# The gather of the special columns behind one more POOL sum, and the three stages of the special frequency two groups later

## The chip, the cores and the metric

The kernel runs on one core of one Trainium2 chip. The core has five engines with instruction queues of their own: TensorE (PE; its weight loads are shown as PEld), VectorE (DVE), ScalarE (ACT), GpSimd (POOL) and SyncE (SP), the last of which only issues DMAs here. Sixteen DMA engines move the data. The metric is the device time of one execution in microseconds (us); smaller is better.

## The reference

One transformer-like block on x of 2048 x 640 in bfloat16, with a spectral filter in place of attention:

```python
mod = (silu(c) @ w_mod).reshape(1, 6, 1, 640)     # sa, ca, ga, sb, cb, gb
h = layernorm(x) * (1 + ca) + sa
X = rfft2(h) * (w_r + 1j * w_i)                   # 2048 x 321 frequencies
x = x + ga * irfft2(X)
h = layernorm(x) * (1 + cb) + sb
x = x + gb * ((silu(h @ w_gate) * (h @ w_up)) @ w_down)   # hidden size 1728
```

## The kernel before, in words

All arithmetic of the two transforms is done as matrix products with tables of cosines and sines. The kernel is one long function; its order of instructions on every engine is the order in which the Python lines run, written out by hand (no planner moves anything). Five parts follow one another:

1. **Forward transform** (up to about 32 us of the profile): layer norm, products with table M (L404) and table R (L413, L415); the result A lies in tile rA.
2. **Join** (about 32 to 60 us): the loop `for g in range(NG + 1)` over 21 groups of column frequencies, four columns each. For group g+2 the function `mix` makes four products (L583) into PSUM, DVE multiplies them with the filter (`prod`, L607, two instructions a group); one or two groups later `stage_b` adds the products up on PE (L615), ACT copies the sum (L618), `stage_c` transforms back in the first step (L645), and ACT or DVE puts the result into tiles Em and Er, which lie in rE (L654). For the odd groups 3 to 17 (`PRE`) POOL adds the two halves of the product first (`presum`, L624, into rE), which halves the work of `stage_b` for that group. Beside these sums POOL adds filter tables (`wsum`, L424) and scales tables for the next part (L785, L791).
3. **Stage one** (about 60 to 80 us): for 16 row tiles t, products of Em and Er with Htab (L728, L737), a copy by ACT (L732), products with RI (L1273, L1276), and a DVE instruction (L1278) that adds x and gives x1. While it runs, the second layer norm of the first two tiles is made (DVE L864), transposed by a DMA (`ln2_tr`, L878, into rW), and scaled and shifted by POOL and ACT (`ln2_mod`, L886, L892).
4. **Gate and up products** of the first chunk of two tiles: `gu13` (L1090, called at t = 15 and waiting for `ln2_mod`), then `gu_plain` (L1102), then the down product (L980).
5. The other three chunks of 4, 4 and 6 tiles, with products saved by Strassen-like sums (L1132, L1003).

**The special frequency.** Rows with frequency 128 times a whole number need a table of their own (Ks). Their path runs through all groups at once. `sp_gather` (L663, nine small POOL additions) collects one element column out of each of the transposed tiles and adds SA, and puts it into B2sp. Then come three stages, each a PE part (`sp_mm`) and an evacuation by DVE (`sp_ev`): stage 0 is three products out of B2sp (L676) and three DVE multiplications (L697); stage 1 is four products (L681) and two DVE copies (L702); stage 2 is four products (L685, L689), two DVE copies (L705), and two DMA stores from SP, L706 and L707, which write row 127 of Em and of Er. Stage one reads that row with its very first product (L728). The three stages use odd g alone, and so the same columns of PSUM that the products of that group leave free.

**Where these stand before the change.** In the loop, `sp_gather` is called at the head of g = 6; on POOL it stands behind the sum for group 7 and ahead of the sum for group 9 (which the loop issues at g = 7). Stages 0, 1, 2 stand at g = 9, 11, 13 (`SPG`): the PE part ahead of the products of group g+2; the DVE part of stages 1 and 2 ahead of the two multiplications of group g+2, that of stage 0 behind them.

**What feeds and follows them.** The gather reads four tiles that DMA transposes fill (L543), issued one after another by SP; the last one writes into rM (columns 64 to 79). Behind the two stores L706 and L707 the SP queue holds, in this order: five loads of the down weights into rA (L822 twice, L824, L825, L826), two small loads of the last gate and up columns (L829, L830), three loads of gate and up weights into rW (L834: gate columns 0 to 511, gate 512 to 1663, up 0 to 511), then the transpose L878 of the second layer norm, and two more up loads (L834). POOL issues a load of gate weights by itself during stage one (L912).

The lines of the loop on which this rests:

```python
        SPG = (9, 11, 13)
        for g in range(NG + 1):
            if g == 6:
                sp_gather()
            if 1 < g < NG - 2:
                if g in SPG:
                    sp_mm(SPG.index(g), g)
                xps = mix(g + 2)
                if g in SPG and SPG.index(g) in (1, 2):
                    sp_ev(SPG.index(g), g)
                prod(g + 2, xps, 0)
                prod(g + 2, xps, 1)
                ...
                if g in SPG and SPG.index(g) not in (1, 2):
                    sp_ev(SPG.index(g), g)
            if g + 2 in PRE:
                presum(g + 2)
```

Of the kernel before, what the change touches and what calls it, by code (L numbers as in the profile page):

```python
# [166 lines left out]
def adaln_block_kernel(ctx, tc, A_x, A_w_r, A_w_i, B_x, B_w_gate, B_w_up, B_w_down, c, w_mod, out):  # L167
# [165 lines left out]
    if True:  # L333
        def bn(ti, n=1, mid=None):
            for i in range(ti, ti + n):
                for k in range(2):
                    nc.vector.bn_stats(bn6a[:, i % 2, k, :], x_sb[:, i, 320 * k:320 * k + 320])  # L337
                    if i == ti + 1 and k == 0 and mid is not None:
                        if mid in (4,6,8):
                            xhat(mid, nc.vector)  # L340
                            xhat(mid + 1, nc.vector)
                        else:
                            xpair(mid)
            for i in range(ti, ti + n):
                nc.vector.bn_aggr(mv[:, i, :], bn6a[:, i % 2])
# [15 lines left out]
        def xpair(lo):  # L361
            nc.gpsimd.tensor_scalar(nmean[:, lo:lo + 2], mv[:, lo:lo + 2, 0], -1.0, 0.0, ALU.mult, ALU.add)
            xhat(lo, nc.gpsimd)
            xhat(lo + 1, nc.vector)

        def xhat(ti, eng):
            o, xi, r = xhs[ti // 2 % 3][:, ti % 2], x_sb[:, ti, :], rstd[:, ti:ti + 1]
            if eng is nc.vector:
                eng.tensor_scalar(o, xi, mv[:, ti, 0:1], r, ALU.subtract, ALU.mult)  # L369
            else:  # L370
                eng.tensor_scalar(o, xi, nmean[:, ti:ti + 1], r, ALU.add, ALU.mult)
# [164 lines left out]
    if True:  # L536
# [22 lines left out]
        def t2_pe(slot):  # L559
            ls = groups[slot] + (groups[4] if slot == 3 else [])  # L560
            n = len(ls)
            tp = banks(slot % 2, 1, [8, 128], BF16)
            for i, l in enumerate(ls):
                nc.tensor.transpose(tp[:, i, :], A_sb[:, l].rearrange("p t k c r -> p (t k c r)"), identb[:])
            B2 = (rM.cut(38400 + 1024 * slot, [n, 128]) if slot < 2 else rM.cut(10240 + 1024 * (slot - 2), [n, 128]))
            if slot == 0:
                nc.scalar.copy(B2[:, 0:2], tp[:, 0:2, :])
                nc.scalar.copy(B2[:, 2:4], tp[:, 2:4, :])
            else:
                nc.scalar.copy(B2[:], tp[:, :n, :])  # L570
            spec.append((B2, 4, slice(ls[0], ls[0] + 4)))
            if n > 4:
                spec.append((B2[:, 4:6], 2, slice(0, 81, 80)))
            for i, l in enumerate(ls):
                B2of[l] = (B2, i)

        def mix(g):
            ls = groups[g]
            n = len(ls)
            xps = banks(2 + 2 * (g % 2), 2, [4, 256])  # L580
            for i, l in enumerate(ls):
                B2, j = B2of[l][0:2]
                nc.tensor.matmul(xps[:, i, 0:192], lhsT=B2[:, j, :], rhs=KS2, start=True, stop=True)  # L583
                if i == 0:
                    for c5 in {8: (0,), 10: (1,), 12: (2,), 14: (3,), 16: (4,), 18: (5, 6), 20: (7, 8, 9)}.get(g, ()):
                        mod_col(psum[:, 3 + 2 * (g % 2), 448 + c5:449 + c5], wm_r[:, :, 1 + c5 // NC5], c5 % NC5)
            return xps
# [11 lines left out]
        def prod(g, xps, hl, v0=0, v1=3):  # L599
            ls = groups[g]  # L600
            n = len(ls)
            if g not in PPs:
                PPs[g] = rM.cut(1536 * (g % 4), [3, 2, NT, 2, n])
            xv = xps[:, :n, 0:192].rearrange("p i (v h k m) -> p v h k m i", v=3, h=2, k=NT)
            st = ls[1] - ls[0]
            in1 = _rev(Wt, (160 - ls[0] if hl else ls[0]) + WP * v0, [[WP, v1 - v0], [321, NT], [160, 2], [-st if hl else st, n]])
            nc.vector.tensor_tensor(PPs[g][:, v0:v1, hl], xv[:, v0:v1, hl], in1, ALU.mult)  # L607
# [53 lines left out]
        def sp_gather():  # L661
            for B2, n, ls in spec:
                nc.gpsimd.tensor_tensor(B2sp[:, ls], B2[:, 0:n, 127], SA[:, ls], ALU.add)  # L663
# [4 lines left out]
        def sp_mm(i, g):  # L668
            b = 2 + 2 * (g % 2)
            if i == 3:  # L670
                for j in range(10):
                    nc.tensor.matmul(psum[:, 1, 320:401], lhsT=SL[:, j // 2, j % 2, :], rhs=Rp[:, j // 2, 81 * (j % 2):81 * (j % 2) + 81],
                                     start=(j == 0), stop=(j == 9))
            elif i == 0:
                for v in range(3):
                    nc.tensor.matmul(gap(81, v, 64, b), lhsT=B2sp[:, 0:81], rhs=Kstab[:, 64 * v:64 * v + 64], start=True, stop=True)  # L676
            elif i == 1:
                for h in range(2):
                    ls = slice(41 * h, 41 + 40 * h)
                    for ps in (1, 0):  # L680
                        nc.tensor.matmul(gap(128, h, ls.stop - ls.start, b), lhsT=PPsp[:, 64 * ps:64 * ps + 128], rhs=identb[0:81, ls],  # L681
                                         start=(ps == 1), stop=(ps == 0))
            elif i == 2:
                for e in range(2):
                    nc.tensor.matmul(gap(128, 0, 1, b), lhsT=Kstab[:, 320 + 128 * e:448 + 128 * e], rhs=Y2sp[:, 80 * e:80 * e + 1],  # L685
                                     start=(e == 0), stop=(e == 1))
                for h, ls in enumerate((slice(1, 40), slice(40, 80))):
                    o = gap(128, h, 40, b)[:, 1 - h:40]
                    nc.tensor.matmul(o, lhsT=Kstab[:, 192:320], rhs=Y2sp[:, ls], start=True, stop=True)  # L689
# [52 lines left out]
        PPs, Y2s, Qs = {}, {}, {}  # L742
        PRE = (3, 5, 7, 9, 11, 13, 15, 17)
        LAGS = range(3, 18)
        SPG = (9, 11, 13)
        t2_pe(0)
        t2_pe(1)
        wsum(0, 16, 8, nc.gpsimd)
# [13 lines left out]
        for g in range(NG + 1):  # L762
            if g == 9:
                nc.gpsimd.tensor_copy(sgnc[:], Kstab[:, 576:577])
            if g == 6:
                sp_gather()
            if 1 < g < NG - 2:
                if g in SPG:
# [6 lines that stand above are left out]
                if g == 2:  # L775
                    wsum(32, 48, 8, nc.gpsimd)
# [4 lines that stand above are left out]
            if g in (10, 12):  # L781
                wsum(64, 80, 8 * (10, 12).index(g), nc.gpsimd)
            if g in (14, 18):
                h4 = slice(4 * (14, 18).index(g), 4 * (14, 18).index(g) + 4)
                nc.gpsimd.tensor_scalar(sgn_H[:, h4, 1], sgn_H[:, h4, 0], sgnc[:, 0:1], 1.0, ALU.mult, ALU.mult)  # L785
            if g == NG - 3:
                nc.vector.tensor_copy(modcols[:, 2, :], psum[:, 3, 448:453])
                nc.vector.tensor_scalar_add(one_p_cb[:], psum[:, 3, 453:458], 1.0)
            if g in (16, 17):
                i = 1 - (16, 17).index(g)  # L790
                nc.gpsimd.tensor_tensor(RI[:, i], RI[:, i], ga_bc[:], ALU.mult)  # L791
            if 0 < g < 3:
                ga_mod(320 * (2 - g), 8 - g)
            for b in (g - 1, g):
                if 0 <= b < NG and (b in LAGS) == (b < g):
                    if b == 4:
                        tp = sp_w()
                        sp_mm(3, 4)
                    Y2s[b] = stage_b(b, PPs.pop(b))
                    if b == 4:  # L800
                        sp_wc(tp)
                        sp_ev(3, 4)
            if g in (7, 9):
                i = (7, 9).index(g)
                turn(64, i, 6 + i, act)
            if g == 0:
                stage_a(3)
            for u, gs in enumerate(units):
                if gs[-1] + (1 if gs[0] >= NG - 2 else 2) == g:
                    stage_c(u)  # L810
                    evac(u)
            if g == NG - 1:
                for c5 in range(NC5):
                    mod_col(psum[:, 3, 192 + c5:193 + c5], wm_r[:, :, 3], c5)
# [596 lines left out]
```

## Time and profile before

| | |
|---|---|
| median of 3 runs | 247.27 us (246.79 to 247.45) |
| the profiled execution's own time | 247.35 us |
| its span, first to last instruction | 245.6 us |
| granted TensorE clock | 0.998 |
| busy: PE, PEld, DVE, ACT, POOL | 236.9, 186.0, 205.5, 170.2, 78.8 us |
| share of the span on the chain that ended last | PE 79%, DVE 7%, POOL 5%, DMA 4% |

An execution takes 1.75 us more than its span. A row of the timeline gives the start in us, the duration in us, the engine, the line, the operation and what it writes and reads, how many instructions are drawn together, and in brackets how long the engine had been idle and what ended that. SP's rows are the issues of DMAs; the data moves later. In the rows of stretches of time, the numbers behind each engine are its busy us in the stretch, and the last two are the mean busy share of the DMA engines (over 1 where several packets are open on one engine) and what they moved in GB/s.

### The profile page before, as it was taken

Reading aid. Unit: us, or ns where it says so; the run is one execution under the profiler, and the core shown is the slowest. Engines: PE = TensorE matmul, PEld = TensorE weight load, DVE = VectorE, ACT = ScalarE, POOL = GpSimd, SP = SyncE. Lnnn points to the kernel's source line nnn. Section 1 sums busy time; section 2 is a strip of 40 time slices with the busy share of each in tenths; the row PEclk is TensorE's granted clock in tenths of the full one; section 3 lists DMA queues with packets and bytes.
Section 4 is the critical chain, followed back from the end, with each engine's and each line's share of the span. In section 5 each row is a group of like instructions: output and inputs, shape, how many; then the busy total and the mean of one; then the engine's idle time right before and its main releaser. Section 6 shows DMA issues by size and latency. Waiting matters only on the chain.

```text
span 245.6 us, 5940 instructions
## 1 busy us (share of the span) xinstructions
PE 236.9 (96%) x2221; PEld 186.0 (76%) x2221; DVE 205.5 (84%) x485; ACT 170.2 (69%) x338; POOL 78.8 (32%) x122
## 2 busy tenths in 40 slices
PE   8899999899999999999999999999999999999994
PEld 2777889799997887788887778887765665666773
DVE  4898988797699995989989968788998777789864
ACT  3898877899997887588864588765247787773220
POOL 3637997698615414002004400001422000004400
PEclk9999999999999999999999999999999999999999
DMA  7999989989999899600005110202411000000111
GB/s 207 373 342 305 349 183 157 261 240 355 327 317 256 166 245 189 138 1 3 0 3 107 56 56 0 56 1 41 91 31 56 0 0 1 3 1 0 56 53 53
DMA packets 44142, 31.19 MB, mean 127 GB/s; under 512 B 21873, under 2 KB 41810, under 8 KB 44114
## 3 DMA queue, kind: packets, MB, share of 16 engines
q1 hardware_dynamic: 42176, 26.15, 41.2%
q0 software_dynamic: 1376, 4.26, 7.6%
q10 hardware_dynamic: 562, 0.41, 0.5%
q8 instruction: 17, 0.28, 0.5%
q14 instruction: 11, 0.09, 0.1%
HBM read 23.49 MB, written 2.62 MB: 106 GB/s over the span
## 4 chain that ended last, share of the span: by engine, by line
PE 79%; DVE 7%; POOL 5%; DMA 4%; issue 3%; ACT 0%; SPq 0%; DVEq 0%; POOLq 0%
PE psum L1132 36%; PE psum L1003 19%; PE psum L1102 6%; PE psum L980 3%; DMA rW<-rL 3%; DVE bn6a L337 3%; PE psum L615 2%; PE psum L583 2%; PE psum L1090 2%; PE psum L404 1%; DMA rX<-in_A_x_dram 1%; DVE rE L369 1%; PE psum L645 1%; POOL rL L1285 1%; DVE rM L607 1%
## 5 line engine op out<-in xcount | busy, mean ns | idle before, releaser
L1132 PEld LDWEIGHTS <-rW 128*128 128x128 bf16 (+1 forms) x429 | 42.0, 98 | 12.6
L1132 PE MATMUL psum<-rW 128*128 128x256 bf16 (+1 forms) x247 | 42.2, 287 | 0.0
L1029 POOL TENSOR_TENSOR rM<-rM,rL 128x320 f32<-128x320 f32 x6 | 5.4, 906 | 96.6 <-ACT rL L1028 96.6
L1003 PEld LDWEIGHTS <-rE 128*128 128x128 f16 (+1 forms) x196 | 19.0, 97 | 7.8
L1003 PE MATMUL psum<-rE 128*128 128x320 f16 (+1 forms) x147 | 22.9, 299 | 0.0
L607 DVE TENSOR_TENSOR rM<-psum,rW 128x384 bf16<-128x384 f32 (+2 forms) x42 | 20.4, 544 | 2.8 <-PE psum L583 2.8
L1170 ACT COPY rX<-psum 128x384 f32<-128x384 f32 (+2 forms) x27 | 14.0, 520 | 7.5 <-PE psum L1132 7.4
L1132 PEld LDWEIGHTS <-rE 128*128 128x128 f16 x156 | 15.3, 98 | 4.7
L1163 ACT COPY rH<-psum 128x384 f32<-128x384 f32 (+2 forms) x27 | 14.0, 517 | 7.0 <-PE psum L1132 6.3
L1167 DVE TENSOR_TENSOR rH<-psum,rM 128x512 bf16<-128x512 f32 (+1 forms) x24 | 15.0, 624 | 4.1 <-PE psum L1132 2.2
L1186 ACT ACTIVATE rL<-psum 128x384 bf16<-128x384 f32 (+2 forms) x27 | 14.4, 533 | 5.4 <-PE psum L1132 3.4
L1171 DVE TENSOR_TENSOR rX<-psum,rX 128x384 f32<-128x384 f32 (+2 forms) x27 | 16.3, 604 | 1.6 <-ACT rX L1170 1.4
L1157 ACT COPY rM<-psum 128x384 f32<-128x384 f32 (+2 forms) x27 | 13.9, 516 | 3.7 <-PE psum L1132 3.7
L1278 DVE SCALAR_TENSOR_TENSOR rM<-psum,rX 128x640 f32<-128x640 f32 x16 | 13.1, 821 | 3.8 <-PE psum L737 2.5
L1132 PE MATMUL psum<-rW,rE 128*128 128x256 bf16 (+1 forms) x78 | 15.6, 290 | 0.0
L1132 PE MATMUL psum<-rE,rY 128*128 128x256 f16 (+1 forms) x78 | 15.6, 290 | 0.0
L1187 ACT ACTIVATE rL<-rX 128x384 bf16<-128x384 f32 (+2 forms) x27 | 15.1, 558 | 0.0
L337 DVE BATCH_NORM_STATS2 bn6a<-rX 128x6 f32<-128x320 bf16 x30 | 13.1, 480 | 2.2 <-DMA rX<-in_A_x_dram 2.2
L1102 PE MATMUL psum<-rW 128*128 128x256 bf16 x130 | 14.4, 273 | 0.0
L972 DVE TENSOR_TENSOR rA<-psum,rM 128x320 bf16<-128x320 f32 (+1 forms) x27 | 12.1, 472 | 2.4 <-PE psum L980 2.3
L1102 PEld LDWEIGHTS <-rW 128*128 128x128 bf16 x130 | 12.7, 98 | 1.4
L424 POOL TENSOR_TENSOR rW<-rW 128x256 bf16<-128x256 bf16 x20 | 13.4, 700 | 0.7 <-DVE rW L393 0.5
(235 smaller groups left out, 640.0 us busy)
## 6 DMA issues: line engine op xcount, KB each, us to landing
rM<-in_w_mod_dram SPq DMA_DIRECT2D x4, 800.0 KB, 8.3
out_dram<-rA SPq DMA_DIRECT2D x31, 80.0 KB, 1.6
rX<-in_A_x_dram SPq DMA_DIRECT2D x6, 320.0 KB, 5.6
rA<-in_B_w_down_dram SPq DMA_DIRECT2D x2, 960.0 KB, 5.4
rY<-in_B_w_gate_dram POOLq DMA_DIRECT2D x2, 832.0 KB, 7.7
rW<-in_B_w_gate_dram SPq DMA_DIRECT2D x1, 1440.0 KB, 10.5
rW<-in_A_w_i_dram SPq DMA_DIRECT2D x2, 642.0 KB, 10.8
rW<-in_A_w_r_dram SPq DMA_DIRECT2D x2, 642.0 KB, 10.2
```

What stands on the lines that cost most here:

```text
L337: nc.vector.bn_stats(bn6a[:, i % 2, k, :], x_sb[:, i, 320 * k:320 * k + 320])
L607: nc.vector.tensor_tensor(PPs[g][:, v0:v1, hl], xv[:, v0:v1, hl], in1, ALU.mult)
L1003: nc.tensor.matmul(o, lhsT=lhs[rows(k), k], rhs=rhs[rows(k), k], start=start and k == ks[0], stop=stop and k == ks[-1], skip_group_check=True)
L1102: nc.tensor.matmul(gu[u], lhsT=Wgu[:, u, c5, ff * 128:(ff + 1) * 128], rhs=h2T[:, :, c5, :], start=(c5 == 0), stop=(c5 == NC5 - 1))
L1132: nc.tensor.matmul(o[:, f], lhsT=w, rhs=b, start=(start and f == 0 and i == 0), stop=(stop and f == len(groups[g]) - 1 and i == len(ops) - ...
L1157: nc.scalar.copy(c0, X)
L1163: nc.scalar.copy(c2, X)
L1167: nc.vector.tensor_tensor(c11, Z, c0, ALU.add)
L1170: nc.scalar.copy(c3, X)
L1171: nc.vector.tensor_tensor(c22, Y, c3, ALU.add)
L1186: nc.scalar.activation(g21, X, ACT.Silu, scale=-1.0)
L1187: nc.scalar.activation(g22, c22, ACT.Silu, scale=-1.0)
```

## The change

`sp_gather` is called at g = 8 instead of g = 6, and the three stages stand at g = 11, 13, 15 instead of 9, 11, 13.

```diff
-                        if mid in (4,6,8):
+                        if mid in (4, 6, 8):
...
-        SPG = (9, 11, 13)
+        SPG = (11, 13, 15)
...
-            if g == 6:
+            if g == 8:
                 sp_gather()
```

The first pair of lines differs in spaces alone. No instruction is added or removed. By the order of instructions on each engine: on POOL the nine additions of the gather go behind one sum (L624, that of group 9) and stay ahead of the copy L764 and the sum of group 11. On PE the three products of stage 0, the four of stage 1 and the four of stage 2 each go two groups back. On DVE the three multiplications L697, the two copies L702 and the two copies L705 each go four multiplications L607 back. ACT's order and SP's order are the same as before; the two stores L706 and L707 keep their place in SP's queue and wait for the copies L705, which come later.

## The prediction

> **What bounds the kernel now.** I read the page first, then the chain of work that ended last, then the timeline of the join engine by engine, and at the end the DMA traffic by stretches. The page: PE is busy nearly throughout, so a microsecond counts where PE stands still.
>
> ```profile
> PE 236.9 (96%) x2221; PEld 186.0 (76%) x2221; DVE 205.5 (84%) x485; ACT 170.2 (69%) x338; POOL 78.8 (32%) x122
> ```
>
> The chain in order of time leaves PE at two places that bear on this change: at the gather (45.2), and at the transpose of the second layer norm (69.5 to 76.6) with POOL's scaling behind it. From 80.2 on it is PE without a break.
>
> ```profile
> 43.96 1.21 issue
> ...
> 45.21 0.97 POOL rE L663 x6
> ...
> 46.23 0.31 PE psum L676 x3
> ...
> 69.49 7.04 DMA rW<-rL
> ...
> 76.72 2.52 POOL rW L886 x4
> 79.27 0.38 PE psum L1090 x2
> ...
> 80.20 14.19 PE psum L1102 x130
> ```
>
> In the timeline of POOL the brackets tell why: the second part of the gather waits for the transpose into rM, and the sums behind it (L624) follow without idle time from 48.16 on.
>
> ```profile
> 43.38 0.58 POOL L663 TENSOR_TENSOR rE<-rL,SA 128x15 bf16<-128x15 bf16 x3
> 45.20 0.97 POOL L663 TENSOR_TENSOR rE<-rM,SA 128x16 bf16<-128x16 bf16 x6 [1.24 <-DMA rM<-rA]
> 46.14 1.15 POOL L624 TENSOR_TENSOR rE<-rM 128x512 bf16<-128x512 bf16 x1
> 47.24 0.18 POOL L764 CAST sgnc<-rE 128x1 f32<-128x1 bf16 x1
> 48.16 1.16 POOL L624 TENSOR_TENSOR rE<-rM 128x512 bf16<-128x512 bf16 x1 [0.74 <-PE psum L583]
> ...
> 53.10 1.16 POOL L624 TENSOR_TENSOR rE<-rM 128x512 bf16<-128x512 bf16 x1
> ```
>
> PE ends its products L645 at 44.81 + 0.55 = 45.36 and stands until the gather is done; L681 (stage 1) and L615 (the sum of group 15) are needed below.
>
> ```profile
> 44.81 0.55 PE L645 MATMUL psum<-Ktab,rY 128*128 128x128 bf16 x7
> 46.23 0.31 PE L676 MATMUL psum<-rE 128*81 128x64 bf16 x3 [0.86 <-POOL rE L663]
> 48.71 0.21 PEld L681 LDWEIGHTS <-rE 81*128 81x128 bf16 x4
> 54.31 0.26 PEld L615 LDWEIGHTS <-rE 128*128 128x128 bf16 x4 [0.16 <-POOL rE L624]
> ```
>
> **The gather and stage 0.** No work is removed or added; only the waits move. At g = 9 PE now goes from L645 straight to the products L583, which need no gather: 0.87 us (45.36 to 46.23) go. On POOL the sum of group 9 comes first. It needs that group's two multiplications on DVE:
>
> ```profile
> 42.55 2.88 DVE L607 TENSOR_TENSOR rM<-psum,rW 128x384 bf16<-128x384 f32 x6
> 46.97 1.02 DVE L607 TENSOR_TENSOR rM<-psum,rW 128x384 bf16<-128x384 f32 x2 [1.54 <-PE psum L583]
> 47.91 0.47 DVE L697 TENSOR_TENSOR rE<-psum,rE 81x64 bf16<-81x64 f32 x3
> ...
> 51.34 0.29 DVE L705 CAST rE<-psum 128x40 bf16<-128x40 f32 x2
> 51.55 1.94 DVE L607 TENSOR_TENSOR rM<-psum,rW 128x384 bf16<-128x384 f32 x4
> ```
>
> The six are groups 8, 9 and 10 at 0.48 each, so group 9 is done at 42.55 + 4 x 0.48 = 44.5 and its sum at 45.65; the gather (0.58 + 0.97, its last input there since 45.20) ends at 47.2. Stage 0 now stands on PE where L681 stood, at 48.71 - 0.87 and a tenth less for the slot of L676 itself: 47.7. So the wait that could take the old one's place has 0.5 us to spare, and I cost it at nothing.
>
> **POOL gives some back.** L764 ends at 47.4, and the sum of group 11, whose multiplications end at 47.99 - 0.9 = 47.1, starts at 47.45 in place of 48.16: 0.71 earlier, not 0.87. POOL is then without idle time up to the sum of group 15, which PE awaits already (0.16 at 54.31). That release comes at 53.6, and PE is there earlier and waits. Gain at the end of the join: 0.71 us.
>
> **Stages 1 and 2.** Their eight products and four DVE copies are the same work two groups later on the same two engines, and each stage keeps its distance of two groups to the one before it, so what it waits for has the same time as before. On PE and DVE I cost this at nothing. The two stores of stage 2 are another matter, because of SP's queue:
>
> ```profile
> 51.77 0.54 SPq L706 DMA_DIRECT2D rE<-rE  x1
> ...
> 53.07 1.12 SPq L822 DMA_DIRECT2D rA<-in_B_w_down_dram  x2
> ...
> 62.97 0.46 SPq L834 DMA_DIRECT2D rW<-in_B_w_up_dram  x1
> ...
> 69.49 1.30 SPq L878 DMA_TRANSPOSE rW<-rL  x1
> ```
>
> The copies L705 now come behind the multiplications of group 16. In the old order those end at 51.55 + 1.94 = 53.49; less about 1.0 for the stall gone and 0.2 for the slot that L705 had ahead of them: start 52.3, end 52.6. L706 goes out 0.14 after it (as 51.77 after 51.63): near 52.7, 0.9 us later by the clock although the join runs earlier. L822 and all the loads behind it start 0.9 later. The stores themselves landed 4.1 after issue at most, so near 57; stage one's first product needs row 127 at 60.12 - 0.71 = 59.4, and 2.4 us are to spare.
>
> ```profile
> rE<-rE SPq DMA_DIRECT2D x1, 16.0 KB, 4.1
> 60.12 1.16 PEld L728 LDWEIGHTS <-rE 128*128 128x128 bf16 x20
> ```
>
> **What the later loads cost.** Nobody needs the weights early, but the transpose L878 is queued behind them, and PE waits for it through POOL. By stretches, DMA share and GB/s last:
>
> ```profile
> 43.00:44.00 1.00, 1.00 (x19) 0.86 (x17) 1.00 (x4) 1.00 (x4) 0.96 (x5) 1.00 1.27 289
> 53.00:55.00 2.00, 2.00 (x39) 1.84 (x37) 2.00 (x6) 1.76 (x4) 2.00 (x3) 1.00 0.46 43
> 55.00:61.00 6.00, 6.00 (x127) 5.87 (x124) 4.61 (x10) 5.46 (x10) 5.30 (x5) 1.00 1.04 358
> 61.00:64.00 3.00, 2.94 (x46) 2.65 (x43) 0.84 (x3) 2.59 (x5) 0.23 (x2) 1.00 1.23 251
> 64.00:72.00 8.00, 8.00 (x114) 7.30 (x112) 7.24 (x19) 7.32 (x17) 4.49 (x7) 1.00 1.08 376
> 72.00:76.50 4.50, 4.50 (x68) 4.20 (x67) 4.20 (x11) 4.29 (x11) 0.00 (x0) 1.00 1.32 145
> ```
>
> The DMA engines run empty at 53 to 55 and are full from 55 to 72. Starting that stretch 0.9 later ends it 0.9 later, so the transpose cannot gain by being issued 0.71 earlier. Whether it loses is not shown: in 72 to 76.5, where it runs, only 145 GB/s move, against 376 before. Those 4.5 us hold 4.5 x (1 - 145/376) = 2.8 us that bandwidth does not explain; the transpose's own 0.33 MB (ten tiles of 128 x 128 in bfloat16) is 1.1 us at the 289 GB/s that another transpose reached. Bounds for its landing: 0.7 earlier (only its issue counts) to 0.9 later (the queue counts in full). I take no shift: a start 0.9 later fits into 2.8 us of slack, and a gain is barred by the queue ahead.
>
> **The sum.** PE waits at L1090 for POOL's scaling already:
>
> ```profile
> PE psum L1090 <- POOL rW L886: 0.6, 1, 0.6
> ```
>
> It arrives 0.71 earlier and finds the transpose landed when it did: the wait grows from 0.6 to 1.3, and from there to the end nothing is touched. Profiled execution 247.35 (span 245.6 and 1.75 around it) - 0.71 + 0.71 = 247.35; the median of the runs is 0.08 lower, so **247.3 us**.
>
> **The rivals.** Under 0.3%, 0.74 us, a change cannot be told from none here.
>
> *Everything moves up* (faster). The transpose's landing follows its issue, the slack of 2.8 us taking up the later queue and more. For it: the slow 72 to 76.5. Against it: a full queue ahead until 72. The gain is the 0.71 of the join: 246.6, a little more if the transpose runs cleaner; PE's remaining wait of 0.6 is the floor, 246.0.
>
> *The stores hold the weights* (slower). SP's wait for L705 is the mechanism; it decides as soon as the transpose lands later than its 69.49 + 7.04 = 76.53. With the full 0.9 it lands at 77.4 and L1090 starts that much later: 248.2. For it: the full DMA engines from 55 on. Against it: the slack.
>
> *Two queues share* (slower still). POOL's own load L912 is issued earlier by the join's 0.7 while SP's last load L834 ahead of the transpose starts 0.9 later, so they overlap more:
>
> ```profile
> DMA packets 949, 1.50 MB, mean 374 GB/s; under 512 B 44, under 2 KB 682, under 8 KB 949
> q1 hardware_dynamic: 725, 0.76, 57.4%
> q0 software_dynamic: 224, 0.74, 54.1%
> ```
>
> From 68 to 72, SP's queue (q1) and POOL's (q0) moved half each, and the transpose's small packets, 44 of them, began just before 72. If both loads, 1.5 MB together, have to be through before them, at 374 GB/s that is 4.0 us from 68.9, the last load's new start: 72.9, a full 1.0 later. With the transpose as slow as before: 248.4. The Trainium skill, page "DMA: Bandwidth & Descriptors", section "Queues, rings and completion order", says that each DMA engine takes turns between the queues it has work for, a packet at a time; the two even shares agree with it, and by that rule a load that joins earlier holds back SP's queue, which the sum above leaves out.
>
> *The gather or row 127 is late after all* (slower): with margins of 0.5 and 2.4 us, small; a miss by 1 us gives 248.3.
>
> **How the numbers follow.** Forecast, within 0.3%: 0.45. Everything moves up: 0.22. The stores hold the weights: 0.20; two queues share: 0.08; late gather or row: 0.05. So faster 0.22, same 0.45, slower 0.33. The range goes from 246.4, just under the first rival's 246.6, to 248.5, just over the third's 248.4; the likeliest case by itself spans 246.6 to 248.0.
>
> **What would show it.** Right: no wait of PE at L676 near 47.7, L624 of group 11 near 47.45, L706 near 52.7 and L822 near 54.0, DMA engines empty a microsecond longer before 56, PE's wait at L1090 grown to about 1.3. Wrong: the transpose landing well before or after 76.5, a wait of PE for L663 at its new place, or L728 waiting for the store.

## The result and the profile after

The changed kernel takes 248.25 us, median of 19 runs (247.47 to 251.62); the kernel before, run beside it, 247.19 us (246.24 to 249.83, 19 runs). The ratio is 1.0061, 95% interval 1.0033 to 1.0088: slower by some 0.6%. The changed kernel's executions are of two kinds, and the numbers below can't be read without that: eleven show a mean granted TensorE clock of 0.998 to 1.0 and take 247.47 to 248.65 us, eight show 0.985 to 0.993 and take 249.24 to 251.62. The profiled execution is one of the eight: 249.94 us, span 248.1, clock 0.991.

The join behaves as the change says. In the timeline of the changed kernel, POOL's gather stands behind the sum of group 9, and nothing waits for it. The weight load of stage 0 (L676) starts at 47.98 without a bracket, and PE's wait of 0.86 us is gone.

```profile
42.18 1.15 POOL L624 TENSOR_TENSOR rE<-rM 128x512 bf16<-128x512 bf16 x1 [0.63 <-DVE rM L607]
...
44.87 1.16 POOL L624 TENSOR_TENSOR rE<-rM 128x512 bf16<-128x512 bf16 x1 [1.26 <-DVE rM L607]
45.98 0.58 POOL L663 TENSOR_TENSOR rE<-rL,SA 128x15 bf16<-128x15 bf16 x3
46.53 0.97 POOL L663 TENSOR_TENSOR rE<-rM,SA 128x16 bf16<-128x16 bf16 x6
47.46 0.18 POOL L764 CAST sgnc<-rE 128x1 f32<-128x1 bf16 x1
47.60 1.15 POOL L624 TENSOR_TENSOR rE<-rM 128x512 bf16<-128x512 bf16 x1
...
52.45 1.16 POOL L624 TENSOR_TENSOR rE<-rM 128x512 bf16<-128x512 bf16 x1
```

The same timeline, PE's weight loads of stage 0 and of stage one's first product:

```profile
47.98 0.21 PEld L676 LDWEIGHTS <-rE 128*81 128x81 bf16 x3
...
59.57 1.16 PEld L728 LDWEIGHTS <-rE 128*128 128x128 bf16 x20
```

Two executions do not begin the join at the same time, so I count from the same product in both: the last small products L440 ahead of the gather. Their first rows, of the kernel before and then of the changed one:

```profile
40.42 0.24 PE L440 MATMUL psum<-identb,rE 16*81 16x16 bf16 x2
```

```profile
40.61 0.24 PE L440 MATMUL psum<-identb,rE 16*81 16x16 bf16 x2
```

From there to the first weight load of stage one (L728) it was 60.12 - 40.42 = 19.70 us and is 59.57 - 40.61 = 18.96: the join gained 0.74 us. That is one pair of executions. What PE waits for at L676 hangs on the transpose into rM, and in the four traces with the old order of all stages (before, and e6, e10 and e12 below) that wait is 0.5 to 0.9 us and the distance to L728 19.37 to 19.72 us; with the new order it is 18.95 or 18.96 in seven traces. So the gain is 0.4 to 0.8 us. All of it, and more, is lost further on. SP's issues in the changed kernel's timeline, with DVE's copies L705 for which the two stores wait:

```profile
53.51 0.54 SPq L706 DMA_DIRECT2D rE<-rE  x1
54.09 0.60 SPq L707 DMA_DIRECT2D rE<-rE  x1
54.80 2.25 SPq L822 DMA_DIRECT2D rA<-in_B_w_down_dram  x2
...
64.36 1.63 SPq L834 DMA_DIRECT2D rW<-in_B_w_up_dram  x1
68.90 2.61 SPq L878 DMA_TRANSPOSE rW<-rL  x1
```

```profile
50.07 1.01 DVE L607 TENSOR_TENSOR rM<-psum,rW 128x384 bf16<-128x384 f32 x2
51.00 0.29 DVE L702 CAST rE<-psum 128x41 bf16<-128x41 f32 x2
51.22 1.94 DVE L607 TENSOR_TENSOR rM<-psum,rW 128x384 bf16<-128x384 f32 x4
53.07 0.29 DVE L705 CAST rE<-psum 128x40 bf16<-128x40 f32 x2
```

The first store goes out at 53.51 (51.77 before), 12.9 us behind L440 where it was 11.35: 1.55 us later. The down weights (L822) follow 1.73 later by the clock. The stretches show what the DMA engines do in the meantime (last two columns: their busy share and GB/s):

```profile
53.00:55.00 2.00, 2.00 (x40) 1.99 (x38) 2.00 (x7) 1.80 (x4) 2.00 (x3) 1.00 0.06 10
55.00:57.00 2.00, 2.00 (x44) 1.95 (x42) 1.97 (x5) 1.79 (x3) 2.00 (x2) 1.00 0.43 54
57.00:63.00 6.00, 5.98 (x114) 5.65 (x112) 3.03 (x7) 5.30 (x11) 2.66 (x3) 1.00 1.05 345
...
64.00:72.00 8.00, 8.00 (x115) 7.32 (x113) 7.12 (x20) 7.32 (x17) 3.91 (x6) 1.00 1.09 350
72.00:74.00 2.00, 2.00 (x32) 1.87 (x30) 2.00 (x7) 2.00 (x5) 0.00 (x0) 1.00 1.31 387
74.00:78.00 4.00, 3.58 (x49) 3.07 (x46) 3.57 (x10) 2.83 (x6) 0.00 (x0) 1.00 1.26 163
```

Before, 55 to 57 was full:

```profile
55.00:57.00 2.00, 2.00 (x42) 1.88 (x39) 1.77 (x4) 1.81 (x3) 2.00 (x3) 1.00 0.97 354
```

In the four microseconds from 53 to 57, 2 x (43 - 10) + 2 x (354 - 54) = 666 KB fewer were moved than before, 1.9 us at the 350 GB/s of the full stretches, and the full stretch ends at 74 instead of 72. The transpose is issued 0.59 earlier and lands later. The chain of work that ended last, in order of time:

```profile
68.90 9.16 DMA rW<-rL
...
78.24 2.17 POOL rW L886 x4
80.41 0.04 issue
80.45 0.58 PE psum L1090 x2
81.04 0.27 PE psum L1273
...
82.10 14.83 PE psum L1102 x130
```

Landed at 78.06 in place of 76.53, and L1102, where PE has no break any more, starts at 82.10 in place of 80.20. The list of waits has for PE:

```profile
PE psum L1090 <- POOL rW L886: 2.0, 4, 1.3
```

Before it was 0.6. And in this execution the wait has a price of its own. By single microseconds, the granted clock is the third number from the end:

```profile
77.00:78.00 1.00, 0.58 (x7) 0.33 (x4) 0.95 (x3) 0.25 (x1) 0.00 (x0) 1.00 1.19 322
78.00:79.00 1.00, 0.16 (x1) 0.19 (x2) 1.00 (x4) 0.60 (x1) 0.76 (x2) 1.00 1.07 344
79.00:80.00 1.00, 0.46 (x3) 0.18 (x2) 0.86 (x5) 0.00 (x0) 1.00 (x3) 0.94 1.09 357
80.00:81.00 1.00, 0.84 (x4) 0.42 (x4) 0.41 (x1) 0.00 (x0) 1.00 (x2) 0.50 1.09 367
81.00:82.00 1.00, 1.00 (x8) 0.78 (x6) 0.00 (x0) 0.38 (x1) 1.00 (x2) 0.50 0.62 206
82.00:83.00 1.00, 1.00 (x7) 0.67 (x6) 0.86 (x3) 0.00 (x0) 1.00 (x3) 0.50 0.69 70
83.00:84.00 1.00, 1.00 (x10) 0.85 (x8) 0.43 (x2) 0.79 (x2) 0.92 (x2) 0.86 0.90 163
```

PE works little from 77.6 to 80, and from about 79.9 to 83.3 it runs at half its clock, 3.4 us. On the chain that costs 1.36 us: from the last L1090 to L1102 it is 82.10 - 80.45 = 1.65 us where it was 80.20 - 79.27 = 0.93, and L1102 takes 14.83 us in place of 14.19. The two kinds of executions lie 2.0 us apart (medians 247.90 of the eleven, 249.89 of the eight); this one trace does not show where the rest comes from.

The loss, then, by profile: the landing comes 1.53 us later by the time of the profile, 1.34 counted from L440, and the end follows it. The 0.74 gained in the join comes to nothing, since PE, which arrives earlier, waits longer. The half clock adds 1.0 to 1.4 in this execution. The eleven executions with the full clock lie 0.7 us above the kernel before (247.90 against 247.19), 0.3%; the rest of the 0.6% comes from the eight.

### The profile page after: what moved, and what is told of

It reads as the page before. It is cut to its first block, busy times and chain, and to the rows that moved or that the text cites. A ratio compares the mean times of both kernels' runs of the same rounds, so it can differ in the third digit from the quotient of the medians.

```text
span 248.1 us, 5939 instructions
## 1 busy us (share of the span) xinstructions
PE 238.1 (96%) x2221; PEld 186.9 (75%) x2221; DVE 206.7 (83%) x485; ACT 170.3 (69%) x338; POOL 78.3 (32%) x122
## 4 chain that ended last, share of the span: by engine, by line
PE 79%; DMA 11%; POOL 3%; SPq 2%; ACT 1%; issue 1%; DVE 1%; ACTq 0%; DVEq 0%; POOLq 0%
PE psum L1132 36%; PE psum L1003 19%; PE psum L1102 6%; DMA rW<-in_A_w_r_dram 4%; DMA rX<-in_A_x_dram 4%; DMA rW<-rL 4%; PE psum L980 3%; PE psum L615 3%; PE psum L583 3%; POOL rW L424 2%; PE psum L645 2%; SPq L266 2%; PE psum L1090 2%; PE psum L728 2%; PE psum L1273 1%; PE psum L1276 1%
## 5 line engine op out<-in xcount | busy, mean ns | idle before, releaser
L607 DVE TENSOR_TENSOR rM<-psum,rW 128x384 bf16<-128x384 f32 (+2 forms) x42 | 20.3, 542 | 2.2 <-PE psum L583 2.0
L1102 PE MATMUL psum<-rW 128*128 128x256 bf16 x130 | 15.0, 280 | 0.0
L1102 PEld LDWEIGHTS <-rW 128*128 128x128 bf16 x130 | 13.1, 101 | 1.8
## 6 DMA issues: line engine op xcount, KB each, us to landing
rW<-in_B_w_gate_dram SPq DMA_DIRECT2D x1, 1440.0 KB, 11.3
```

Source lines behind the costliest of these rows:

```text
L1102: nc.tensor.matmul(gu[u], lhsT=Wgu[:, u, c5, ff * 128:(ff + 1) * 128], rhs=h2T[:, :, c5, :], start=(c5 == 0), stop=(c5 == NC5 - 1))
```

## The experiments

The theory: SP issues its DMAs in the order of its queue, the two stores in it now wait longer for L705, and the loads and the transpose behind them pay (the prediction's second rival). Against it stand POOL's load L912, which the faster join brings forward (the third rival), the granted clock, and something in the join itself. Experiments named "before" start from the kernel before, the others from the changed one. All ratios are to the kernel before, run beside them on the same chip. "Third stage" is stage 2, and a line number is a few lower or higher where the edit adds or removes lines above it.

A reading that helps with all of them: counted from L440, the end of the span lies 168.7 to 168.9 us behind the start of POOL's scaling L886 in ten of the nineteen traces (before: 76.72 - 40.42 = 36.30 and 245.6 - 40.42 = 205.18, so 168.88), with stores early or late, and with or without a wait of PE at L1090. In nine of those ten the chain that ended last runs through the transpose, so that its landing decides the time, in the kernel before too; in the tenth, e7, it does not, and PE has no wait. Where L886 starts earliest or PE lost time elsewhere, the distance is longer (169.1 in e12, 169.4 in e6, 170.3 in e10). Worked out from the traces, in us from the first L440 (in the changed kernel the half clock lies between L886 and the end, hence 169.9); L834 is the largest load ahead of the transpose, 1440 KB:

| kernel | store L706 issued | load L834 lands | transpose L878 issued | lands | L886 starts | span ends |
|---|---|---|---|---|---|---|
| before | 11.4 | 29.6 | 29.1 | 36.1 | 36.3 | 205.2 |
| changed | 12.9 | 32.5 | 28.3 | 37.4 | 37.6 | 207.5 |
| e7, stores early | 5.4 | 28.2 | 28.3 | 34.7 | 34.9 | 203.7 |
| e12, before, stores early | 5.4 | 28.7 | 29.0 | 35.1 | 35.3 | 204.4 |
| e5, load first | 12.8 | 28.9 | 28.3 | 35.4 | 35.6 | 204.5 |
| e6, before, load first | 11.3 | 29.3 | 29.9 | 35.7 | 35.9 | 205.3 |
| e13, load first, stage 2 at 14 | 11.9 | 28.6 | 28.5 | 35.0 | 35.2 | 204.1 |
| e2, before, stage 2 at 15 | 13.2 | 31.7 | 28.9 | 36.9 | 37.1 | 206.0 |
| e3, stage 2 at 14 | 12.0 | 30.9 | 28.5 | 37.4 | 37.6 | 206.3 |
| e14, before, stage 2 at 14 | 11.8 | 30.0 | 28.5 | 36.5 | 36.7 | 205.4 |
| e4, twelve products ahead of L1090 | 12.9 | 31.1 | 28.3 | 36.4 | 36.6 | 205.4 |
| e8, without POOL's load | 12.9 | 31.1 | 28.3 | 35.5 | 35.7 | 204.5 |
| e10, before, without POOL's load | 11.0 | 29.3 | 28.7 | 33.7 | 33.9 | 204.1 |
| e16, POOL's load late | 12.9 | 31.3 | 28.4 | 35.6 | 35.7 | 205.4 |

The table has two steps. The first is the theory's: where the stores stand ahead of all the loads, L834 lands the later, the later they go out (29.3 to 29.6 with stores at 11.0 to 11.4, 30.0 to 30.9 at 11.8 to 12.0, 31.1 to 32.5 at 12.9 and later), and it lands early, at 28.2 to 29.3, where the stores or a load go ahead of them. The second step, from there to the landing of the transpose, is 6.4 to 6.5 us in the kernel before, in e3 and e14 and in the five kernels with stores early or a load first, 4.9 to 5.3 in the changed kernel, e4 and e2, and 4.3 to 4.4 without POOL's load in the way (e8, e10, e16). So what a short hold adds to L834's landing reaches the transpose in full (e3, e14), and what a longer one adds only in part; why the second step is shorter behind late stores, the traces do not show.

**Stores out of SP's way, first try.** ACT issues them at the end of g = 15.

```diff
-                nc.sync.dma_start(Em[127:128]...)
-                nc.sync.dma_start(Er[127:128]...)
+        def sp_store():
+            nc.scalar.dma_start(Em[127:128]...)
+            nc.scalar.dma_start(Er[127:128]...)
...
+            if g == 15:
+                sp_store()
```

> The changed kernel with the two stores L706 and L707 taken out of SP's queue: ACT issues them at the end of group 15. Theory (the stores hold the weights: SP waits for L705 ahead of all the loads): the five loads of rA go out at once behind L556, near 45 in place of 54.8, the transpose lands by 74, PE's wait at L1090 is gone, and with the 0.7 us of the join the time is 245.5 to 246.6. Rival (POOL's load L912 and SP's last load overlap): the load L834 starts when it did, since it waits for PE's L645 near 59, so half of the loss stays, 247 to 248. Rival (the cost sits in the join or in the clock itself): 248.2 as the changed kernel.

Measured: 255.85 us, ratio 1.0352 (1.0322 to 1.0382). ACT's timeline and the waits tell of a trap: the second store went out 7.4 us after the first, and ACT's next copy waited all that time.

```profile
53.13 0.54 ACTq L708 DMA_DIRECT2D rE<-rE  x1
60.58 0.48 ACTq L709 DMA_DIRECT2D rE<-rE  x1
61.16 0.58 ACT L618 CAST rY<-psum 128x512 bf16<-128x512 f32 x1 [7.47 <-DMA rA<-in_B_w_down_dram]
```

The release named is a load of down weights that SP had issued. The trace's semaphore numbers tell why: the DMAs of SP and ACT use the same eight completion semaphores in turn, POOL's use others, and number 100, for which the second store waits, was that of SP's 80 KB load L829, issued at 50.95. The move cost the join 7 us and says nothing on the theory.

**Third stage alone.** The kernel before with its last stage two groups later: the stores come late, the join gains nothing.

```diff
-        SPG = (9, 11, 13)
+        SPG = (9, 11, 15)
```

> The kernel before with stage 2 alone moved from g = 13 to 15; gather and stages 0 and 1 stay, so the stall of 0.87 us at L676 stays too. Theory (the stores hold the weights): L706 goes out near 54, over 2 us later than before, the transpose lands 2 us later, near 78.6, and the time is 248.8 to 250.5, worse than the changed kernel because the join gains nothing. Rival (the gather's new place costs): 247.2 as before. Rival (POOL's load and SP's last load overlap): as the theory in direction, 248 to 249.

Measured: 247.78 us, ratio 1.0043 (1.0021 to 1.0064). The stall at L676 stays (0.7 us), the stores are 1.8 us later, the landing 0.8. Late stores alone make the kernel slower, but by 0.9 us where the theory had asked for 1.6 and more.

**Third stage one group earlier in the changed kernel.**

```diff
-        SPG = (11, 13, 15)
+        SPG = (11, 13, 14)
```

> The changed kernel with stage 2 one group earlier, at g = 14. Theory (the stores hold the weights): L706 goes out 1.0 us earlier than in the changed kernel, the transpose lands about 1.0 earlier, near 77, PE's wait at L1090 is below 1.5 us and the clock does not fall: 247.0 to 247.5. Rival (the gather's new place or the join costs): 248.2 as the changed kernel.

Measured: 248.19 us, ratio 1.0049 (1.0026 to 1.0072), a miss: it is the time of the rival. The stores come only 0.6 us later than before, but the loss stays, and by the table the transpose lands as late as in the changed kernel, by the longer second step.

**The clock.** Twelve, then thirty, products without use on PE ahead of the products that wait.

```diff
+                idle2(12)
                 fin13 = gu13(0, at_of(0))
```

> The changed kernel with twelve idle products of 256 columns (about 1.3 us) on PE right ahead of L1090; they lie in the wait there. Theory (part of the runs are slower because PE idles at L1090 and its clock is then granted at half): no execution below a clock of 0.997, all times between 247.4 and 248.7, median 247.9. Rival (the slow clock has another cause): times from 247.5 to 251 with clocks down to 0.985 as in the changed kernel.

> The changed kernel with thirty idle products (3.2 us) on PE ahead of L1090, as long as the longest wait there. Theory (the slow runs come from PE idling at L1090): no run with a clock below 0.997; PE is free for L1090 near 80.5, when the late transpose lets it start anyway, so all runs lie between 247.8 and 248.9. Rival (the clock falls for another reason): some runs above 249 with clocks of 0.993 and less.

Measured: with twelve 248.13 us, ratio 1.0051 (1.0023 to 1.0078), and two of twelve runs at a clock of 0.991 to 0.992 (250.66 and 251.23); with thirty 249.28 us, ratio 1.0078 (1.0056 to 1.0099), all five at 1.0, one of which took 1397.5 us for a reason that nothing here shows and is not in the ratio. That work for PE keeps the clock up is likely but not shown: at eight of nineteen, five executions without a fall would come by chance once in some fifteen tries. Thirty products cost more than they save, and with twelve the ten executions at the full clock (median 247.86) still lie 1.0 us above the kernel before: the clock adds to the loss and is not its cause. It belongs to the change all the same: of the 110 executions of the kernel before, run beside these experiments, that took less than 250 us, one shows 0.992 and none less.

**A load ahead of the stores.** The first half of the down weights (960 KB) is issued at g = 10, ahead of the stores, in the changed kernel and in the one before.

```diff
+            if g == 10:
+                nc.sync.dma_start(Wd_sb[:, 0:6, :], B_w_down[0:768, :]...)
...
-    for h in range(2):
+    for h in range(1, 2):
```

> The changed kernel with the first of the two loads L822 (960 KB) moved ahead of the two stores in SP's queue; everything else as it was. Theory (SP's wait for L705 keeps the DMA engines empty from 52 to 56, and the transpose lands late by that): the engines carry this load from 52 to 55, all that follows ends 2.6 us earlier than in the changed kernel, the transpose lands near 75.5, PE's wait at L1090 is gone and no run has a low clock: 245.9 to 246.6. Rival (POOL's load overlaps with SP's last load and that is the cost): SP's last load is done earlier than POOL's starts, so it predicts a gain too, but below 1 us: 247.2 to 247.8. Rival (the cost is elsewhere): 248.2.

> The kernel before with the same load moved ahead of the stores. Theory: the empty stretch of the DMA engines, 53 to 55 there, is filled, the transpose lands 1 to 2 us earlier and PE's wait of 0.6 at L1090 goes, while the stall of 0.87 at the gather stays: 246.2 to 246.7 against 246.9 to 247.2, so 0.7 us slower than the changed kernel with this load moved. Rival (nothing of this binds in the kernel before): 247.

Measured: changed 246.23 us, ratio 0.9975 (0.995 to 1.0), as the theory had it; before 246.68 us, ratio 0.999 (0.9971 to 1.001). The DMA engines now have work while SP waits; the stretches of e5:

```profile
53.00:55.00 2.00, 2.00 (x42) 2.00 (x39) 2.00 (x5) 1.80 (x4) 2.00 (x3) 1.00 1.04 332
55.00:57.00 2.00, 2.00 (x45) 1.96 (x42) 1.85 (x7) 1.79 (x4) 2.00 (x3) 1.00 0.66 153
```

The same edit takes 2.0 us off the changed kernel (248.25 to 246.23) and 0.3 off the one before, which is not clear of noise, although the stores still go out 12.8 us behind L440. That is the strongest evidence for the theory: what costs is not the stores' lateness but the idle DMA engines behind them.

**Stores early.** Both stores are issued at g = 6 from a constant tile, so SP never waits for L705 (the stores at the old place are taken out); row 127 of the two tables holds constants in place of the special frequency, in both kernels.

```diff
+            if g == 6:
+                nc.sync.dma_start(Em[127:128]..., identb[:, 0:64].unsqueeze(1))
+                nc.sync.dma_start(Er[127:128]..., identb[:, 64:80])
```

> The changed kernel with both stores issued near 45, ahead of all these loads, out of a table that is there (row 127 of Em and Er gets a constant in place of the special frequency; the stages 0 to 2 still run). SP then waits for nothing in the join. Theory: the loads of rA follow the others without an empty stretch, the transpose lands by 75, PE does not wait at L1090: 245.6 to 246.3, the lowest of all. Rival (POOL's load): between 247 and 247.8. Rival (elsewhere): 248.2.

> The kernel before with both stores issued near 45 out of a table that is there (row 127 of Em and Er gets a constant in place of the special frequency); SP waits for nothing in the join. The changed kernel so took 245.88. Theory: with SP's wait out of both, only the join is left, and this kernel is slower by the 0.7 us that the join gains: 246.4 to 246.8. Rival (the gain of the join is never there): 245.9.

Measured: changed 245.88 us, ratio 0.9959 (0.994 to 0.9978); before 246.06 us, ratio 0.9963 (0.995 to 0.9976). Without SP's wait the changed kernel loses nothing, and PE shows no wait at the scaled transpose. The kernel before gains from it too, more than expected: it was already paying for the stores. The two traces end 203.7 and 204.4 us behind L440, 0.7 apart, which is the gain of the join; the medians are 0.2 apart, and with their intervals the changed kernel may be anything from 0.7 us faster to 0.5 slower, so the runs do not show that gain by themselves.

**POOL's load.** Both kernels without the first load at L912; a part of one table of gate weights is left out, so the result lacks it.

```diff
-            if t in (8, 11):
-                gu_dma(GS[0][:], B_w_gate, t // 11 * 2, 2, t == 8)
+            if t == 11:
+                gu_dma(GS[0][:], B_w_gate, 2, 2, True)
```

> The changed kernel without POOL's first load L912 of 832 KB (the first half of the gate part of one table is left out, and the second load overwrites in place of adding). Rival (POOL's load L912 shares the engines with SP's last load): the transpose lands 2 us earlier, 76, and the time is 246.3 to 246.8. Theory (SP's wait for L705): the transpose still starts behind SP's last load, at 71.5 to 72.5, and lands near 76.5 to 77: 247.0 to 247.6, so more than half of the loss stays.

> The kernel before without POOL's first load L912 (the same part of one table is left out). Without it the changed kernel took 246.58. Theory (SP's wait costs in the changed kernel, and the load only fills what the wait left): here the transpose is hardly late, the wait at L1090 of 0.6 goes, the stall of 0.87 stays: 246.2 to 246.6, so without the load the two kernels stand within 0.4 of each other. Rival (the cost is the overlap with POOL's load): without the load the change shows its gain of the join, so this kernel is 0.7 slower than 246.58: 247.2.

Measured: changed 246.58 us, ratio 0.998 (0.9964 to 0.9997); before 246.13 us, ratio 0.996 (0.9947 to 0.9972). The first time is the rival's, not the theory's (247.0 to 247.6); the second refutes the rival, which had 247.2. Both get faster: the load stands in the way of the transpose in either. The changed kernel stays the slower one by 0.2 points, at the edge of the noise. The traces say more: without the load the transpose still lands 1.8 us later in the changed kernel (35.5 against 33.7) with stores 1.9 us later, so the hold behind the stores does not need this load. The time shows little of it because in e10 nothing on the chain waits for the transpose any more (170.3 from L886 to the end, 1.4 us more than where the landing decides).

**Stores behind POOL's sum of group 17**, issued by POOL itself and taken out of SP's queue.

```diff
+        def sp_store():
+            nc.gpsimd.dma_start(Em[127:128]...)
+            nc.gpsimd.dma_start(Er[127:128]...)
...
+            if g == 15:
+                sp_store()
```

> The changed kernel with the two stores issued by POOL, behind its sum for group 17, and nothing left out; SP waits for nothing in the join. Theory (SP's wait for L705 costs): as with the stores near 45, 245.6 to 246.4, unless POOL's two issues, about 1 us each, put off L791 and L785, which stage one needs: then up to 1 us more, 247.4. Rival (the cost is POOL's load alone): 247 to 248.

Measured: 250.43 us, ratio 1.0131 (1.0098 to 1.0163), a miss on both sides; five of its six executions show a clock of 0.985 to 0.993, and the profiled one is the sixth, 248.51 us. SP's loads now go out from 44.8 on, and the stores come into full DMA engines: 6.5 us to land, and PE waits for row 127 (L730 there, L728 elsewhere). The DMA issues and the waits of that kernel:

```profile
rE<-rE POOLq DMA_DIRECT2D x1, 16.0 KB, 6.5
```

```profile
PE psum L730 <- DMA rE<-rE: 2.6, 1, 2.6
```

So there is a bound on the other side: with too much ahead of them the stores are late for stage one. One load of 960 KB ahead (e5) is within it.

**One group instead of two.** The first is the kernel before with only the third stage one group later; the second has the load ahead of the stores and the stage at 14.

```diff
-        SPG = (9, 11, 13)
+        SPG = (9, 11, 14)
```

> The kernel before with the third stage of the special frequency behind group 14 instead of 13: the join's wait at L676 stays, only the two stores come later, by one group of DVE (in the run with the stage behind group 15 they came 1.84 us later against the join's first L440, and the time was 0.43% above the one of before). If the loss comes from the hold behind the stores in proportion to their lateness: stores some 0.9 us later, half of that loss, 0.1 to 0.4% above before, that is 247.3 to 248.0 us beside a before of 247.1. If the hold costs nothing up to a point and then a fixed amount (a step): either no difference (within 0.1%) or the full 0.4% and more, 248.1 us.

> The changed kernel with the first half of the down weights loaded ahead of the two stores, and the third stage behind group 14 instead of 15. Without the load ahead, the stage behind group 14 won nothing back (ratio 1.0049 against 1.0061 with group 15). If the hold behind the stores is the only cause of the loss, the load ahead hides it here as it did with group 15 (246.23 us, ratio 0.9975), and the stage a group earlier costs nothing of its own: 245.9 to 246.4 us, ratio 0.995 to 0.998. If the third stage behind group 14 costs something by itself (on PE or DVE between groups 13 and 15, by which the join's gain shrinks from 0.74 to 0.53 us in that profile, or more): 246.7 us or above, ratio 0.999 or more.

Measured: before with 14: 248.37 us, ratio 1.0073 (1.0046 to 1.01), four of twelve runs at a clock of 0.993; the other eight have a median of 248.1, 0.5% above the kernel before. That is the second of its two cases. The load first and 14: **245.88 us, ratio 0.9956 (0.9941 to 0.9972)**, with no fall of the clock. It computes everything and beats both kernels: 0.44% faster than the one before, and its median is 2.4 us below that of the changed one. Its chain:

```profile
68.65 6.44 DMA rW<-rL
75.13 0.15 issue
75.28 2.53 POOL rW L888 x4
77.85 0.38 PE psum L1092 x2
```

So the stage's place at 14 costs nothing by itself once the DMA engines are busy. But e14 loses, within the noise, as much with stores some 0.5 us later as the whole change does, so the loss is not in proportion to the stores' lateness. e14's profiled execution is the fastest of its twelve (247.49), and its trace does not show what the others lost.

**POOL's load held back.** In e14's trace the join is 0.5 us faster, because the wait at L676 is 0.3 us in that execution, and it brings L912 0.5 us forward (26.6 instead of 27.1 behind L440). Four small copies on POOL hold it back; in the changed kernel and in e13 five multiplications done again hold it back behind the transpose's issue.

```diff
+                for _ in range(4):
+                    nc.gpsimd.tensor_copy(warm[:], st2[:, 0, 0:1])
```

```diff
+            if t == 8:
+                for c5 in range(NC5):
+                    nc.gpsimd.tensor_scalar_mul(gdiag[:, c5], identb[:], modcols[:, 3, c5:c5 + 1])
             if t in (8, 11):
                 gu_dma(GS[0][:], B_w_gate, t // 11 * 2, 2, t == 8)
```

> The kernel before with the third stage behind group 14, as in the last call (248.37 us, ratio 1.0073, with the stores 0.4 us later and POOL's load at L912 0.5 us earlier against the join's first L440), and four small copies of POOL in front of that load, 0.18 us each, so that it is issued as late as in the kernel before (27.1 us behind L440). If the loss comes from POOL's load, which now goes ahead of SP's last loads on the shared DMA engines: back to 247.0 to 247.4 us, ratio 0.998 to 1.002. If it comes from the later stores alone: 248.0 to 248.6 us, ratio 1.004 to 1.009, as without the copies.

> The changed kernel with POOL's first load at L912 held back until some 5 us later, behind five more multiplications of POOL (done again, with the same result) that wait for PE's second product at L1264. Without that load the changed kernel took 246.58 us (ratio 0.998). If the load's place ahead of the transposes is what makes the landing late: 246.2 to 246.9 us, ratio 0.996 to 1.000. If the hold behind the stores decides by itself: 247.8 to 248.5 us, ratio 1.003 to 1.007. A loss beyond that would be the load's own lateness: what is added to it at the second L912 then comes late.

> The fastest kernel so far (first half of the down weights ahead of the stores, third stage behind group 14: 245.88 us, ratio 0.9956) with POOL's first load held back in the same way. That kernel shows no wait of PE at L1090, so the transposes are early enough: 245.7 to 246.2 us, ratio 0.994 to 0.998, no gain. If the landing still sets the end there: 245.2 to 245.6 us, ratio 0.992 to 0.994.

Measured: e15 247.73 us, ratio 1.0041 (1.0022 to 1.0061); e16 247.38 us, 1.0022 (1.0009 to 1.0036); e17 246.78 us, 1.0000 (0.9986 to 1.0013). By its time e15 lies between its two cases, by its ratio at the lower edge of the second, "the later stores alone" (the copies held the load back further than meant, to 28.5 us behind L440); its interval overlaps that of e14, and in its trace the transpose lands no earlier (36.7 behind L440, 36.5 in e14). e16 lies between its two cases, e17 above both of its own. Two of e16's twelve executions, at clocks of 0.992 and 0.986, took 251.87 and 252.65 us. In e16 the transpose lands 1.8 us earlier than in the changed kernel with equally late stores, but the load is then late for what is added to it (POOL's second L912 waits 2.0 us for it, 3.5 in e17), and in both traces PE waits 0.7 us for DVE at the down product, which it does in neither of the kernels they start from. So the load's place has a share in the landing; how large a share of the change's loss it is, these runs do not separate.

## Why the prediction was wrong

Forecast 247.3 with "no change" likeliest; measured 248.25, inside the range, on the slower side. Point by point:

- **The stall at L676 and the gather**: right. The wait is gone, stage 0 found its input there (47.98; forecast 47.7), and the join gained 0.74 us against 0.71 forecast. That the two lie so close is partly luck of the execution: the gain is 0.4 to 0.8 us over the traces.
- **POOL gives some back**: right. Sum of group 9 until 46.03 (45.65 forecast), sum of group 11 at 47.60 (47.45), sum of group 15 until 53.61 (53.6). The changed kernel's join begins 0.19 later by the clock, which is part of each difference.
- **Row 127**: right. The second store landed 3.8 us after 54.09, at 57.9, 1.7 us ahead of L728.
- **L705 "start 52.3, end 52.6"**: mis-sized by 0.8 us. I took 1.0 us for the stall and 0.2 for L705's slot off the end of group 16's multiplications. They ended at 51.22 + 1.94 = 53.16 instead of 53.49, 0.33 earlier: DVE, which waits on the way there for PE (0.37 and 0.54 us at L583) and for a sum of POOL (0.16 at L624), had only part of the join's gain by then. So the stores were 1.74 us later by the clock, not 0.9.
- **"I take no shift: a start 0.9 later fits into 2.8 us of slack"**: the step that failed. I read the low rate of 72 to 76.5 as slack of the transpose, and so let PE's wait for it grow by the join's gain alone. It is not slack: with the stream ending two microseconds later the slow stretch comes two microseconds later (74 to 78 at 163 GB/s, where 72 to 76.5 had 145), and the landing 1.34 us later from L440. Of the packets under 512 B, which are small as the transpose's are, 1315 of the 1330 from 71 to 77 came after 72 before, and 1253 of the 1344 from 72 to 79 after 74 in the changed kernel: the transpose ends the stream; it hardly runs beside it. The table shows that the landing decided the time in the kernel before too, where I had quoted the wait of 0.6 us at L1090 and still took a later queue to leave the landing where it was.
- **The stores hold the weights**: this rival happened. Its time, 248.2, is the measured one, partly by luck: it had the stores 0.9 late with the full delay, against 1.55 late with a landing 1.34 later, and no lower clock. e5, e7 and e13 show the mechanism by taking it away. Its proportion, every microsecond of the stores one of the landing, does not hold: 0.5 to 0.6 us of the stores gave 0.4 and 1.3 of the landing in e14 and e3, and 1.8 gave 0.8 in e2.
- **Two queues share**: in part. POOL's load does stand in the transpose's way (e8, e10, e16), but in the kernel before as well, and without it the transpose is still 1.8 us later. The Trainium skill's rule that I had set beside it, that each DMA engine takes turns between its queues (page "DMA: Bandwidth & Descriptors", section "Queues, rings and completion order"), agrees with e16: with POOL's load out of the way, the transpose landed 7.2 us after its issue instead of 9.2.
- **Everything moves up**: it needs SP without the wait; then it is what e7 and e13 do.
- **Not foreseen**: the granted clock, which falls in eight of the nineteen executions of the changed kernel.

Open: why stores 0.5 to 0.6 us later (e14, e3) cost about as much as stores 1.5 and 1.8 us later (the changed kernel, e2). The intervals of the four ratios overlap, so their order is not shown; the table puts the difference into the step from L834 to the landing and does not say what shortens it. The landings of single executions scatter by half a microsecond and more (36.4 to 37.4 behind L440 in e4, e11 and the changed kernel, whose stores are equally late), and there is one profile for each kernel.

## What to carry to other kernels

Before moving a step, ask which of its instructions stand in an in-order DMA queue, and price not their own delay but the idle time of the DMA engines behind them; a low rate ahead of a landing is slack only if the landing comes no later when the stream ends later. A load issued ahead of a waiting store fills that idle time: here it turned a change that lost 0.6% into one that gains 0.25%, at the edge of the noise, and 0.4% with the third stage one group earlier. And a short wait on the chain can mark a bound: in the kernel before the wait of only 0.6 us at L1090 meant that the landing already decided the time.

## What the hardware showed unexpectedly

- The granted clock fell to 0.50 after a stretch in which PE was not idle for long: its waits at L1090 were 1.26, 0.27, 0.27 and 0.16 us with a product between each, from 77.6 to 80.5, and it fell at 79.9, before the last of them. It was whole again some 3.4 us later. The Trainium skill, page "TensorE: Matmul & The Clock Gate", section "Part 1: The HAM clock gate (the "warmup" mystery)", gives about 3.4 us of sustained work for the way up, which agrees, and an idle window of about 3.4 us for the way down; the longest idle time here is 1.26 us, so on that side the measurement differs. With the same sum of waits, 2.0 us, the clock stayed at 1.00 in e3's profiled execution: it differs from execution to execution.
- Two engines that issue DMAs are not independent in a program like this: a 4 KB store on ACT waited 7.4 us for a weight load of SP with which it shared a completion semaphore (number 100 in the trace of e1).
- A 16 KB store landed 2.3 us after its issue when the DMA engines were nearly idle (the changed kernel) and 6.5 when they were full (e9).
